# The last output tile of a gated attention and GLU kernel ends with its 128 columns instead of its 384, and the 384 leave through the phi tasks' buffer

## The chip, the cores and the metric

The kernel runs on one core of a Trainium2 chip. The metric is the device time of one execution in microseconds (us); it is shown as the median of three runs. Five engines work side by side: TensorE (PE, matrix products into PSUM), VectorE (DVE), ScalarE (ACT), GpSimd (POOL) and SyncE (SP). In this kernel SP only issues DMAs and waits for them.

## The reference

The input is `x`, 2048 tokens of width 512. The output is a mix of two branches with one gate per token:

```python
g = sigmoid((x * gate_w).sum(-1, keepdims=True))
a = attention(x)                                  # 32 heads, 4 segments of 512 tokens, see below
b = (gelu(x @ w_gate) * (x @ w_up)) @ w_down      # inner width 1792
return g * a + (1 - g) * b
```

In each segment, each head computes causal softmax attention, and a second answer read from a memory `M`, `z` summed over the earlier segments with `phi(t) = t+1 if t>0 else exp(t)`. The two are mixed by `sigmoid(beta)`, and all heads go through `wo`. All inputs and the output are bf16.

## The kernel before

The 2048 tokens are four segments `s` of 512, and each segment is four tiles of 128 tokens. A Python planner lists the work as tasks. Each task is a short run of instructions on one engine, with the buffers that it reads and writes. The order of the tasks on each engine is written out by hand in `ORDER` (lines 46 to 136), one string per engine, SP among them. The planner then plays this order with an estimated duration per instruction (`est`, and `issue` for a DMA). That play decides only two things: in which of the four `psW` PSUM banks a matmul group is placed, and in which sequence the tasks are entered when the semaphore waits are worked out. A wait that an engine has already made for the same count or a later one is dropped (lines 377 to 393).

The tasks at the end of the program, with their names:

- `downs(s)` (line 1023) makes the output of a segment. For a tile it adds up 14 matmuls with `wd` over the GLU's hidden columns `hT`, and 4 with `wo` over the attention's `oT`, into one PSUM bank. The evacuation `fin` multiplies by `omgt`, which is `1 - g` per token, into one of three staging buffers `ost`, and the DMA `out<tile>` on SP writes these 128 KB to memory. Tiles are numbered 0 to 15 over the sequence; the last segment makes 12 to 15. In its tiles 0 to 2 the `wd` part runs first, in pieces of two matmuls: `D3_2.14` and `D3_2.16` are the last two pieces of tile 14.
- Tile 15 is different (`on_x`, line 1028). Its 512 columns are split in 384 (`u = 0`) and 128 (`u = 1`), which are accumulated in the PSUM banks `X[0]` and `X[1]` (`psXALL` in the profile) that the attention no longer needs. The pieces are `D3_3w0.*` and `D3_3w1.*` for `wd`, 14 matmuls each in pieces of four (the last, `.12`, has two), and `D3_3a0.0` and `D3_3a1.0` for `wo`, four matmuls each.
- `fin3_30` (line 1048) evacuates the 384 columns on ACT into `ost[0]`, and `out15_0` writes them, 96 KB. `ost[0]` was last filled by tile 12, so `fin3_30` also waits until `out12` has landed. `fin3_31` (line 1051) evacuates the 128 columns on DVE into `obf`, and `out15_1` writes them, 32 KB in rows of 256 bytes.
- `fin3_2` (ACT, line 1065) evacuates tile 14 for `out14`. `fin3_1` (DVE, line 1068) does tile 13.
- `pex` (line 439) holds 128 x 1024 bf16. It is the scratch of the `phi_task`s (line 689), which compute `exp` for `phi`. Its last user is `pqc3_1` on DVE, for the fourth segment's queries.
- After its last DMA, SP waits for the semaphore of each output write (line 1140): those of tiles 0 to 14, then `sem_tail`, which belongs to `out15_0`, then that of `out15_1`.

In the order before, SP issues `out12 out13 out15_1 out14 out15_0`, ACT runs `fin3_0 fin3_2 fin3_30`, and DVE runs `fin3_1 fin3_31`.

Of the kernel before, what the change touches and what calls it, by code (L numbers as in the profile page):

```python
# [26 lines left out]
N_OST = 3  # L27
# [60 lines left out]
    "act": (  # L88
# [47 lines left out]
}  # L136
GAP = {DVE: 0.012, POOL: 0.063}
HOP = {PE: 0.25, ACT: 0.07, DVE: 0.07, POOL: 0.10, SP: 0.0}
# [272 lines left out]
def act_t(n, psum=True, ap=False):  # L411
    return (0.167 if psum else 0.20) + n / 1200.0 + (0.093 if ap else 0.0)


def dve_t(n, mode=1, psum=False, ap=False):
    return max(0.19, 0.155 + n / mode / 960.0 + (0.06 if ap else 0.0))
# [11 lines left out]
def _build(es, nc, A_x, A_wq, A_wk, A_wv, A_wo, A_beta, B_w_gate, B_w_up, B_w_down, gate_w, out):  # L428
    def sb(name, shape, dtype=BF):
        return es.enter_context(nc.sbuf_tensor(name, shape, dtype))  # L430
# [8 lines left out]
    pex = sb("pex", [P, 2, 512])  # L439
# [33 lines left out]
    ostage = [sb(f"ost{i}", [P, 512]) for i in range(N_OST)]  # L473
# [19 lines left out]
    def sem(name):  # L493
        nsem[0] += 1
        return es.enter_context(nc.semaphore(f"{name}_{nsem[0]}"))
# [3 lines left out]
    def task(name, eng, instrs, **kw):  # L499
        return S.add(Task(name, {eng: instrs}, **kw))  # L500

    def mm(g, view, lhsT, rhs, reads, first, last, n, fkey=None):
        return Instr(lambda e: e.matmul(view(), lhsT, rhs, start=first, stop=last),  # L503
                     reads=reads, writes=[fkey if fkey is not None else g.key], est=mm_t(n))

    def pieces(name, g, instrs, size, after=(), bias=0.0):

        r = None
        for i in range(0, len(instrs), size):
            r = task(f"{name}.{i}", PE, instrs[i:i + size], grp=g, after=after, bias=bias)  # L510
        return r
# [12 lines left out]
    def dma(name, eng, out_ap, in_ap, reads, writes, nbytes, issue=0.5, transpose=False, bias=0.0, sm=None,  # L524
            nonc=False, after=()):
        sm = sm if sm is not None else sem("d")

        def f(e):
            if transpose:
                return e.dma_start_transpose(out_ap(), in_ap())  # L530
            if nonc:
                with nc.allow_non_contiguous_dma(reason="small vector"):
                    return e.dma_start(out_ap(), in_ap())
            return e.dma_start(out_ap(), in_ap())
        return task(name, eng, [Instr(f, reads, writes, issue, dma_sem=sm)], bias=bias, nbytes=nbytes, after=after)
# [58 lines left out]
    for nm, u, k0, nk, c0 in (("0a", 0, 0, 1, 0), ("0b", 0, 1, 1, 1024), ("1", 0, 2, 2, 2048),  # L594
# [8 lines left out]
        dst = xT[0][:, k0:k0 + nk, 256 * u:256 * u + 256]  # L603
# [419 lines left out]
    def downs(s):  # L1023
        sl = s % 2
        last = s == NSEG - 1
        for tile in range(4):
            gt = 4 * s + tile
            on_x = last and tile == 3
            att = [(oT[sl][:, kb, tile * 128:(tile + 1) * 128], wo[:, kb, :], [("oT", sl, tile, kb), ("w", "wo")])
                   for kb in range(4)]  # L1030
            dwn = [(hT[sl][:, fb, tile * 128:(tile + 1) * 128], wd[:, fb, :], [("hT", sl, fb), ("w", ("wd", fb // 7))])
                   for fb in range(NFT)]
            dep = fins if on_x else ()
            if on_x:
                for part in (dwn, att):
                    for u in range(2):
                        c0, cn = 384 * u, (384, 128)[u]
                        ins = [mm(None, lambda u=u, cn=cn: X[u][:, 0:cn], a, b[:, c0:c0 + cn], rd,
                                  part is dwn and i == 0, part is att and i == 3, cn, fkey=("X", u))
                               for i, (a, b, rd) in enumerate(part)]  # L1040
                        pieces(f"D{s}_{tile}{'wa'[part is att]}{u}", None, ins, 4, after=dep)
                for u in range(2):
                    c0, cn = 384 * u, (384, 128)[u]
                    dst, dk = (ostage[(4 * s + tile) % N_OST][:, 0:cn], ("ost", (4 * s + tile) % N_OST)) if u == 0 else \
                        (obf[:, 0:cn], ("obf",))
                    rd = [("X", u), ("omgt", s)]
                    if u == 0:
                        task(f"fin{s}_{tile}{u}", ACT, [Instr(lambda e, dst=dst, u=u, cn=cn, gt=gt: e.activation(  # L1048
                            dst, X[u][:, 0:cn], ACTF.Copy, scale=omgt[:, gt:gt + 1]), rd, [dk], act_t(cn, ap=True))])
                    else:  # L1050
                        task(f"fin{s}_{tile}{u}", DVE, [Instr(lambda e, dst=dst, u=u, cn=cn, gt=gt: e.tensor_scalar(
                            dst, X[u][:, 0:cn], omgt[:, gt:gt + 1], None, ALU.mult), rd, [dk], dve_t(cn, ap=True))])
                    dma(f"out{gt}_{u}", SP, lambda gt=gt, c0=c0, cn=cn: out[0, gt * 128:(gt + 1) * 128, c0:c0 + cn],
                        lambda dst=dst: dst, [dk], [("hbm", gt, u)], 256 * cn, sm=sem_out[gt] if u else sem_tail)
                continue
            g = Grp(banks)
            key = g.key
            view = lambda g=g: g.f32()[:, :]
            seq = dwn + att if last else att + dwn
            ins = [mm(g, view, a, b, rd, i == 0, i == len(seq) - 1, 512, fkey=key)  # L1060
                   for i, (a, b, rd) in enumerate(seq)]
            pieces(f"D{s}_{tile}", g, ins, 2, after=dep)
            rd = [key, ("omgt", s)]
            f = S.add(Task(f"fin{s}_{tile}", {
                ACT: [Instr(lambda e, view=view, gt=gt, tile=tile: e.activation(
                    ostage[(4 * s + tile) % N_OST][:], view(), ACTF.Copy, scale=omgt[:, gt:gt + 1]), rd,
                    [("ost", (4 * s + tile) % N_OST)], act_t(512, ap=True))],
                DVE: [Instr(lambda e, view=view, gt=gt, tile=tile: e.tensor_scalar(  # L1068
                    ostage[(4 * s + tile) % N_OST][:], view(), omgt[:, gt:gt + 1], None, ALU.mult), rd,
                    [("ost", (4 * s + tile) % N_OST)], dve_t(512, ap=True))]}, grp=g))  # L1070
            if s == NSEG - 2:
                fins.append(f)
            dma(f"out{gt}", SP, lambda gt=gt: out[0, gt * 128:(gt + 1) * 128, :],
                lambda tile=tile: ostage[(4 * s + tile) % N_OST][:], [("ost", (4 * s + tile) % N_OST)], [("hbm", gt)], 131072, sm=sem_out[gt])

    fins = []
    sem_out = [sem("so") for _ in range(16)]
    sem_tail = sem("st")
# [17 lines left out]
    attention(1)  # L1096
    ups(0)
    downs(0)
    xdma(3)
    prep(2)  # L1100
    gelu_phase(1, [], [2])
    memory(2)
    attention(2)
    ups(1)
    downs(1)
    prep(3)
    gelu_phase(2, [], [3])
    attention(3)
    ups(2)
    downs(2)  # L1110
    ups(3)
    downs(3)
# [75 lines left out]
```

## Time and profile before

| what | value |
|---|---|
| time, median of 3 runs | 266.68 us (266.48 to 266.70) |
| profiled execution, its time | 266.81 us |
| profiled execution, its span | 265.1 us |
| DVE, ACT, POOL busy | 197.6, 209.0, 105.9 us (75%, 79%, 40%) |
| instructions on PE (matmuls, and as many weight loads) | 3153 |
| output writes | 15 of 128 KB, one of 96 KB, one of 32 KB |

The span is the stretch that the profiler shows; the time of the same execution is 1.71 us longer. In the views, a row of the timeline has its start, its duration, the engine, the source line, the operation, what it writes and what it reads, the number of instructions merged in the row, and, in brackets, how long the engine sat idle before it and which work ended that. Matmuls are recorded at line 503, whatever the task, so the tasks are told apart by their tiles and by the number in a row. Matmuls overlap, and their ends are modelled; the chain of waits gives each row of matmuls the time from the end of the one before. The issue of a DMA is a row of the SP queue, and "us to landing" counts from the start of that row.

### The profile page before, as it was taken

The page shows a single profiled execution, that of the slowest core. Times are in us where ns is not written, and L with a number is a line of the kernel's source. Part 1 is how long each engine was busy: PE and PEld are TensorE (multiplying, and loading weights), DVE is VectorE, ACT ScalarE, POOL GpSimd, SP SyncE. Part 2 cuts the span into 40 slices and gives each one's busy share as a digit, 9 for nine tenths or more (in the row PEclk, how much of TensorE's full clock was granted, in tenths as well). Part 3 has the DMA queues.
Part 4 walks back from the last instruction along what each step waited for, and adds up shares of the span by engine and source line. Part 5 has one row for each costly group of instructions (what it writes and reads, how often), then busy time and mean ns, then how long its engine had stood idle before and what let it go on. Part 6 is the DMA issues. An engine that isn't in the chain of part 4 may idle for free.

```text
span 265.1 us, 7394 instructions
## 1 busy us (share of the span) xinstructions
PE 261.1 (98%) x3153; PEld 117.5 (44%) x3153; DVE 197.6 (75%) x376; ACT 209.0 (79%) x179; POOL 105.9 (40%) x256
## 2 busy tenths in 40 slices
PE   8999999999999999999999999999999999999995
PEld 4644444344444434443544434444444433444453
DVE  0778788999997968889897776879887742466651
ACT  3698988998999788799867977878787777777611
POOL 8206686352600077174400365609470117362400
PEclk9999999999999999999999999999999999999999
DMA  7972118900003894420004251200000021301002
GB/s 224 309 182 53 33 24 197 240 4 0 2 19 102 243 160 79 63 82 0 2 0 68 67 131 21 83 2 20 5 2 0 2 63 42 79 2 42 22 0 82
DMA packets 32769, 18.25 MB, mean 69 GB/s; under 512 B 20576, under 2 KB 32736, under 8 KB 32736
## 3 DMA queue, kind: packets, MB, share of 16 engines
q1 hardware_dynamic: 31632, 16.73, 27.0%
q10 hardware_dynamic: 1104, 1.05, 1.2%
q8 instruction: 25, 0.41, 0.7%
q14 instruction: 8, 0.07, 0.1%
HBM read 9.84 MB, written 2.10 MB: 45 GB/s over the span
## 4 chain that ended last, share of the span: by engine, by line
PE 96%; ACT 1%; DMA 1%; issue 0%; ACTq 0%
PE psW L503 75%; PE psXALL L872 9%; PE psW L920 6%; PE psXALL L503 3%; PE psW L928 1%; DMA hT<-in_A_x_dram 1%; PE psW L839 1%; ACT pt L878 1%; PE psXALL L792 1%; PE psXALL L599 1%; ACT L878 0%; ACT ost L1048 0%; ACTq L399 0%
## 5 line engine op out<-in xcount | busy, mean ns | idle before, releaser
L878 ACT ACTIVATE pt<-psXALL 128x2048 bf16<-128x2048 f32 x64 | 120.1, 1876 | 27.0 <-PE psXALL L872 23.5
L881 POOL TENSOR_SCALAR_AFFINE_SELECT pt<-pt 128x256 bf16<-128x256 bf16 x128 | 58.9, 472 | 102.9 <-ACT pt L878 98.1
L503 PE MATMUL psW<-xT,wu 128*128 128x512 bf16 x224 | 55.3, 380 | 0.0
L503 PE MATMUL psW<-xT,wg 128*128 128x512 bf16 x224 | 54.2, 380 | 0.0
L503 PE MATMUL psW<-wd,hT 128*128 128x512 bf16 x210 | 54.1, 380 | 0.0
L1019 DVE TENSOR_TENSOR hT<-psW,hT 128x512 bf16<-128x512 f32 x56 | 36.8, 683 | 16.5 <-PE psW L503 16.2
L881 POOL TENSOR_SCALAR_AFFINE_SELECT ptl<-ptl 128x512 bf16<-128x512 bf16 x32 | 22.5, 704 | 38.0 <-ACT ptl L878 36.4
L503 PEld LDWEIGHTS psW<-xT,wu 128*128 128x128 bf16 x224 | 20.3, 98 | 25.7 <-issue 2.7
L503 PEld LDWEIGHTS psW<-xT,wg 128*128 128x128 bf16 x224 | 20.6, 98 | 24.7 <-issue 2.1
L934 DVE STREAM_TRANSPOSE tb<-psW 128x512 f32<-128x512 f32 x32 | 21.5, 699 | 11.7 <-PE psW L928 11.5
L503 PEld LDWEIGHTS psW<-wd,hT 128*128 128x128 bf16 x210 | 19.3, 98 | 23.9 <-issue 3.0
L872 PE MATMUL psXALL<-qT,kpad 32*128 32x320 bf16 (+3 forms) x512 | 25.4, 273 | 0.0
L1003 ACT ACTIVATE hT<-psW 128x512 bf16<-128x512 f32 x28 | 15.7, 596 | 5.5 <-PE psW L503 5.4
L503 PE MATMUL psW<-xT,wk 128*128 128x512 bf16 (+1 forms) x80 | 19.0, 342 | 0.0
L920 PE MATMUL psW<-pt,vaug 128*17 128x192 bf16 (+3 forms) x512 | 18.8, 273 | 0.0
L872 PEld LDWEIGHTS psXALL<-qT,kpad 32*128 32x128 bf16 x512 | 7.6, 92 | 24.5 <-ACT pt L878 15.4
L503 PE MATMUL psW<-wv,xT 128*128 128x512 bf16 x64 | 18.5, 380 | 0.0
L878 ACT ACTIVATE ptl<-psXALL 128x2048 bf16<-128x2048 f32 x8 | 15.0, 1876 | 3.9 <-PE psXALL L872 3.6
L503 PE MATMUL psW<-wo,oT 128*128 128x512 bf16 x60 | 17.0, 380 | 0.0
L1068 DVE TENSOR_SCALAR ost<-psW,omgt 128x512 bf16<-128x512 f32 x9 | 6.7, 746 | 11.9 <-PE psW L503 11.9
L520 DVE CAST hT<-psW 128x512 bf16<-128x512 f32 x19 | 12.8, 684 | 3.7 <-PE psW L503 3.5
L779 POOL COPY exsT<-exs 32x4 f32<-32x4 f32 x64 | 13.8, 216 | 3.6
(104 smaller groups left out, 302.2 us busy)
## 6 DMA issues: line engine op xcount, KB each, us to landing
out_dram<-ost SPq DMA_DIRECT2D x15, 128.0 KB, 1.9
wg<-in_B_w_gate_dram SPq DMA_DIRECT2D x2, 896.0 KB, 7.5
wu<-in_B_w_up_dram SPq DMA_DIRECT2D x2, 896.0 KB, 7.3
wd<-in_B_w_down_dram SPq DMA_DIRECT2D x2, 896.0 KB, 7.4
phkt<-in_A_x_dram SPq DMA_DIRECT2D x3, 512.0 KB, 4.5
vlow<-vaug SPq DMA_DIRECT2D x8, 136.0 KB, 2.8
hT<-in_A_x_dram SPq DMA_DIRECT2D x2, 256.0 KB, 3.9
wq<-in_A_wq_dram SPq DMA_DIRECT2D x2, 256.0 KB, 5.4
```

Of the source, the lines that this page charges most:

```text
L503: return Instr(lambda e: e.matmul(view(), lhsT, rhs, start=first, stop=last), reads=reads, writes=[fkey if fkey is not None else g.key], e ...
L520: alts[DVE] = [Instr(lambda e: e.tensor_copy(dst(), src()), reads=reads, writes=writes, est=dve_t(n))]
L599: task(f"x0t{nm}_{u}", PE, [Instr(lambda e, k=k, a=a, u=u, k0=k0, src=src: e.transpose(src[:, k, a * 128:(a + 1) * 128], xin[:, 2 * u + a, ...
L779: cross = task(f"exsT{s}", POOL, [Instr(lambda e, g=g, c=c: e.tensor_copy(exsT[sl][32 * g:32 * g + 32, c:16:4], exs[32 * c:32 * c + 32, s4 ...
L872: instrs.append(Instr(lambda e, g=g, lhs=lhs, rhs=rhs, c0=c0, ncol=ncol: e.matmul(X[g][:, c0:c0 + ncol], lhs(32 * g), rhs(32 * g), start=T ...
L878: exp_task(s, f"exp{s}_{t}{name}", [Instr(lambda e: e.activation(dst[:], XALL[:, :].rearrange("p (g c) -> p g c", g=4), ACTF.Exp, scale=AT ...
L881: task(f"msk{s}_{t}{name}", POOL, [Instr(lambda e, view=view, pat=pat, base=base: e.affine_select(out=view, in_=view, compare_op=ALU.is_ge ...
L920: instrs.append(Instr(lambda e, t=t, q=q, kb=kb, slot=slot, c0=c0: e.matmul(gp.f32()[32 * q:32 * q + 17, 128 * kb + 64:512], Vaug[sl][:, k ...
L934: task(f"pvt{s}_{t}_{j}", DVE, [Instr(lambda e: e.transpose(Tb[:, j, :], gp.f32()[:, :]), [gp.key], [("Tb", j)], dve_t(512))], grp=gp)
L1003: lambda e, g=g, ft=ft, s=s: e.activation(hT[s % 2][:, ft, :], g.f32()[:, :], ACTF.Gelu_apprx_tanh),
L1019: task(f"Um{s}_{ft}", DVE, [Instr(lambda e, g=g, ft=ft: e.tensor_tensor(hT[sl][:, ft, :], g.f32()[:, :], hT[sl][:, ft, :], ALU.mult), [g.k ...
L1068: DVE: [Instr(lambda e, view=view, gt=gt, tile=tile: e.tensor_scalar(ostage[(4 * s + tile) % N_OST][:], view(), omgt[:, gt:gt + 1], None, ...
```

## The change

Four things are changed.

1. On PE, the end of the order. Behind `D3_2.14` stood the last ten matmuls of the 128 columns' `wd` part, then `D3_2.16`, `D3_3a1.0`, `D3_3w0.12` and `D3_3a0.0`. Now `D3_2.16` comes first, then the rest of the 384 columns (`D3_3w0.12`, `D3_3a0.0`), then the rest of the 128 columns (`D3_3w1.4`, `.8`, `.12`, `D3_3a1.0`).
2. On SP, the end of the order: `out14`, `out15_0`, `out15_1` in place of `out15_1`, `out14`, `out15_0`.
3. `fin3_30` writes the first 384 columns of `pex` instead of `ost[0]`, and `out15_0` reads them there.
4. The planner's estimate for the issue of an output write is 0.35 us instead of 0.5.

The orders of ACT, DVE and POOL are the same, and so is each instruction's size.

```diff
         "D3_0.4 D3_0.6 qk3_3B0 U3_11.2 D3_1.2 D3_0.8 U3_12.0 U3_12.2 qk3_3A1 D3_0.10 D3_1.4 pv3_2_1 pv3_2_0 "
         "qk3_3B1 D3_1.6 D3_1.8 D3_0.12 D3_0.14 D3_1.10 D3_1.12 pv3_3_0 pv3_3_1 D3_1.14 D3_3w1.0 D3_2.0 D3_3w0.0 "
-        "D3_2.2 D3_2.4 D3_3w0.4 D3_3w0.8 D3_0.16 D3_2.6 D3_2.8 D3_1.16 D3_2.10 D3_2.12 D3_2.14 D3_3w1.4 D3_3w1.8 "
-        "D3_3w1.12 D3_2.16 D3_3a1.0 D3_3w0.12 D3_3a0.0 "),
+        "D3_2.2 D3_2.4 D3_3w0.4 D3_3w0.8 D3_0.16 D3_2.6 D3_2.8 D3_1.16 D3_2.10 D3_2.12 D3_2.14 D3_2.16 D3_3w0.12 "
+        "D3_3a0.0 D3_3w1.4 D3_3w1.8 D3_3w1.12 D3_3a1.0 "),
...
-        "oTd3_3 out10 out9 out11 out12 out13 out15_1 out14 out15_0 "),
+        "oTd3_3 out10 out9 out11 out12 out13 out14 out15_0 out15_1 "),
...
-                    dst, dk = (ostage[(4 * s + tile) % N_OST][:, 0:cn], ("ost", (4 * s + tile) % N_OST)) if u == 0 else \
+                    dst, dk = (pex[:, 0, 0:cn], ("pex",)) if u == 0 else \
                         (obf[:, 0:cn], ("obf",))
...
-                        lambda dst=dst: dst, [dk], [("hbm", gt, u)], 256 * cn, sm=sem_out[gt] if u else sem_tail)
+                        lambda dst=dst: dst, [dk], [("hbm", gt, u)], 256 * cn, issue=0.35, sm=sem_out[gt] if u else sem_tail)
...
-                lambda tile=tile: ostage[(4 * s + tile) % N_OST][:], [("ost", (4 * s + tile) % N_OST)], [("hbm", gt)], 131072, sm=sem_out[gt])
+                lambda tile=tile: ostage[(4 * s + tile) % N_OST][:], [("ost", (4 * s + tile) % N_OST)], [("hbm", gt)], 131072, issue=0.35, sm=sem_out[gt])
```

## The prediction

> **What bounds the kernel now.** I read the page first: its head, the busy times, and the engines' shares of the chain of waits.
>
> ```profile
> span 265.1 us, 7394 instructions
> PE 261.1 (98%) x3153; PEld 117.5 (44%) x3153; DVE 197.6 (75%) x376; ACT 209.0 (79%) x179; POOL 105.9 (40%) x256
> PE 96%; ACT 1%; DMA 1%; issue 0%; ACTq 0%
> ```
>
> PE works for 261.1 of 265.1 us and holds 96% of the chain. No matmul is removed, so the change can gain only behind the last one. Hence the second view, the end of the chain in order of time (start, duration, what, how many).
>
> ```profile
> 256.98 3.02 PE psW L503 x14
> 260.01 0.56 PE psXALL L503 x10
> 260.56 0.43 PE psW L503 x2
> 261.00 1.21 PE psXALL L503 x10
> 262.21 0.02 issue
> 262.23 0.04 ACTq L399
> 262.27 0.05 issue
> 262.31 0.58 ACT ost L1048
> ```
>
> The four matmul rows are, by the written order: 14 of 512 columns ending with `D3_2.14`; the ten of 128 columns (`D3_3w1.4` to `.12`), 56 ns each; the two of `D3_2.16`, 215 ns each; and ten mixed ones, `D3_3a1.0` (four of 128 columns), `D3_3w0.12` and `D3_3a0.0` (six of 384). At 56 ns the four take 0.22, which leaves 0.99/6 = 0.165 us for one of 384. PE is done at 262.21, ACT evacuates from 262.31 to 262.89. What follows is in the timeline of the same stretch, on the SP queue alone, in the DMA view (KB, us to landing), and in SP's final waits.
>
> ```profile
> 261.12 0.69 ACT L1065 ACTIVATE ost<-psW,omgt 128x512 bf16<-128x512 f32 x1 [2.89 <-PE psW L503]
> 261.26 0.35 DVE L1051 TENSOR_SCALAR obf<-psXALL,omgt 128x128 bf16<-128x128 f32 x1 [1.69 <-PE psXALL L503]
> 261.64 0.33 SPq L534 DMA_DIRECT2D out_dram<-obf  x1
> 262.01 0.43 SPq L534 DMA_DIRECT2D out_dram<-ost  x1
> 262.92 0.33 SPq L534 DMA_DIRECT2D out_dram<-ost  x1
> out_dram<-ost SPq DMA_DIRECT2D x1, 96.0 KB, 1.6
> out_dram<-obf SPq DMA_DIRECT2D x1, 32.0 KB, 1.4
> L1141 SPq EVENT_SEMAPHORE  x8: 27/28/28, 263.3 to 264.6; - x8
> ```
>
> SP issues `out15_0` at 262.92, 0.03 behind ACT's end. It lands 1.6 later, at 264.52, and SP's last wait (27 to 28 ns) is at 264.6. The program then closes until 265.1, so 0.58 lies behind the landing. From PE's end the tail is 0.10 + 0.58 + 0.03 + 1.6 + 0.58 = 2.89 us. The 128 columns, meanwhile, are evacuated at 261.26 and wait for nobody: their write lands at 261.64 + 1.4 = 263.04, 1.5 us before it is needed.
>
> **The change, part by part.**
>
> *PE's order.* The same 22 matmuls follow 260.01. `D3_2.16` runs to 260.44, the six of 384 columns to 261.43, and the fourteen of 128 at 56 ns to 262.21. Nothing is gained or lost on PE: the operands are old (the last write of `oT`, the second row below, ends at 256.35), and each group stays in its bank. The unknown is whether fourteen short matmuls in a row keep the pace of ten. The bound from below is 56 ns; the one from above is a weight load that isn't covered, 98 ns by the first row below, which for the four added ones makes 4 x 0.042 = 0.17 us. I take zero, because the run of ten is the nearest row.
>
> ```profile
> L503 PEld LDWEIGHTS psXALL<-wd,hT x11: 97/98/98, 259.8 to 261.1; 128*128 128x128 bf16 x11
> 255.93 0.42 DVE L954 TENSOR_TENSOR oT<-oT,ott 128x512 bf16<-128x512 bf16 x1
> ```
>
> The Trainium skill speaks against this order: "TensorE: Matmul & The Clock Gate", section "Back-to-back issue gap", gives about 81 ns for each matmul of 128 columns in a sustained stream with weight loads. By it, an estimate, PE would be 14 x 25 ns = 0.35 us later; the run of ten measured 56 ns, so the trace does not agree, and the sum goes without it.
>
> *The last evacuation.* It passes from ACT to DVE. DVE's `fin3_31` began at 261.26, 0.04 behind the end of `D3_3a1.0` (261.00 + 0.22), and takes 0.35. In place of 0.10 + 0.58 that is 0.39, a gain of 0.29. The two hops differ because ACT's row has a wait of its own in the queue (0.04) and DVE's hasn't; nothing in `fin3_31`'s waits changes. If DVE's hop were ACT's, the gain would be 0.23. After: 262.21 + 0.39 = 262.60, issue at 262.63 with the same 0.03.
>
> *The last write.* 32 KB in 1.4 us instead of 96 KB in 1.6: gain 0.2, and 0.1 to 0.3 with the rounding of both. SP's last wait is now the one for the last landing, where before one more stood behind it: 0.03 for that row, at most 0.08 with the gap to 264.6; I take 0.05.
>
> Here, too, the skill warns: "DMA: Bandwidth & Descriptors", section "Specifications", has writes under 512 bytes a descriptor done by read-modify-write, and these rows are 256 bytes. The rates below bear the direction out (94 GB/s at a share of 0.43 against 197 at 0.61), yet the whole 32 KB still landed earliest.
>
> ```profile
> 262.40:262.75 0.35, 0.00 (x0) 0.00 (x0) 0.00 (x0) 0.35 (x1) 0.00 (x0) 1.00 0.43 94
> 263.70:264.20 0.50, 0.00 (x0) 0.00 (x0) 0.00 (x0) 0.00 (x0) 0.00 (x0) 1.00 0.61 197
> ```
>
> *What is moved ahead must be out of the way.* Three issues now stand in front of `out15_1` on SP. `fin3_2` starts 0.12 behind 260.44 as it did behind 261.00, ends at 261.25, and `out14` is issued from 261.28 to 261.71 at the longer 0.43. `fin3_30` starts by 261.53, ends by 262.11, and `out15_0` is issued from 262.14 to 262.47, or 262.57 at 0.43. `out15_1` is ready at 262.63: SP is free with 0.06 to 0.16 to spare. That slack is the cover of the two issues; a delay of `fin3_30` beyond it costs one for one. `out15_0` lands at 263.74 and `out15_1` at 264.03, so the later landing is the 32 KB.
>
> *The idle buffer.* The issue rows of `out12` and `out13`, each with its time to landing:
>
> ```profile
> 258.25 0.33 SPq L534 DMA_DIRECT2D out_dram<-ost  x1
> out_dram<-ost SPq DMA_DIRECT2D x1, 128.0 KB, 3.9
> 259.60 0.33 SPq L534 DMA_DIRECT2D out_dram<-ost  x1
> out_dram<-ost SPq DMA_DIRECT2D x1, 128.0 KB, 2.9
> L702 DVE TENSOR_TENSOR phq<-phq,pex x1: 694/694/694, 175.3 to 175.3; 128x1024 bf16<-128x1024 bf16 x1
> ```
>
> `out12` lands at 262.15. In `ost[0]`, `fin3_30` could not start before that, 0.62 later than it now may, and SP would hold `out15_1` behind `out15_0` (262.15 + 0.10 + 0.58 + 0.03 + 0.33 = 263.19 instead of 262.63, +0.56: the whole gain). `pex` was last read at 175.3 + 0.69, before work that ACT has waited for since, so its new wait costs nothing. Before, this wait was hidden by 0.06 us under PE's end; moving to `pex` alone gains no more than that.
>
> *The planner's 0.35.* It issues no instruction. It could only move a group to another bank in the middle, where an eviction is 0.69 (ACT) or 0.75 us (DVE) long. I take zero, with bounds of minus and plus 0.7: the output writes do not set the planned start of any task on another engine but `fin3_30`, so I expect the same program up to 260.01.
>
> **Sum.** 0.29 + 0.20 + 0.05 = 0.54 us. The tail is 0.39 + 0.03 + 1.4 + 0.53 = 2.35 instead of 2.89, and the span 264.56. The profiled execution's 266.81 becomes 266.27; it lies 0.13 above the median of 266.68, which becomes **266.14**. A measurement of this kernel can tell about 0.2% from no change, 0.53 us, so the line is at 266.15 and the forecast almost on it.
>
> **The rivals.**
>
> *The writes collide on SP or in the DMA engines* (chance 0.08). `out15_1` follows 96 KB by 0.49. For it: SP's slack of 0.06 is thin. Against it: `out10` and `out9`, twice 128 KB and 0.4 apart, landed in 1.7 to 1.8.
>
> ```profile
> L534 SPq DMA_DIRECT2D out_dram<-ost x2: 337/384/431, 241.5 to 241.9; - x2
> DMA to landing us min/median/max: 1.7/1.8/1.8
> ```
>
> A landing of 1.8 instead of 1.4 gives 266.54; a tenth lost in SP's queue gives 266.24.
>
> *The short matmuls slow down* (0.06). Unhidden loads on the four added ones give 266.14 + 0.17 = 266.31; by the skill's rate, that of 81 ns on all fourteen, it would be 266.49.
>
> *Slower: a late DMA engine catches the last write* (0.06). The two slow landings have a cause in these windows of the DMA queues and of the engines:
>
> ```profile
> q8 instruction: 1, 0.02, 55.2%
> 259.20:260.90 1.70, 1.70 (x18) 1.11 (x17) 0.37 (x1) 0.00 (x0) 0.00 (x0) 1.00 0.43 136
> 260.90:262.10 1.20, 1.20 (x11) 0.65 (x9) 0.35 (x1) 0.69 (x1) 0.00 (x0) 1.00 0.06 14
> 262.10:262.40 0.30, 0.09 (x1) 0.00 (x0) 0.00 (x0) 0.09 (x1) 0.00 (x0) 1.00 0.00 0
> ```
>
> One instruction packet between 259.1 and 259.3 takes 55.2% of 16 engines for 0.2 us, that is 1.77 us of one engine; then about one engine (0.06 of 16) drags 14 GB/s behind it until 262.1. If that happened under `out15_1`, a landing of 2.9 like `out13`'s gives 266.14 + 1.5 = 267.64. It costs time from a landing of 1.4 + 0.54 = 1.94 on. Against it: the packet comes before the first changed instruction, and the drag is over at 262.1, half a us ahead of the new last issue.
>
> *The plan shifts after all* (0.04): some banks in the middle change, 265.4 to 266.8.
>
> **How the numbers follow.** The forecast has 0.76. Its own range, from the 0.23 of the hop, the 0.1 to 0.3 of the landing and the spread of the three runs (0.2), is 265.95 to 266.35. Being on the line it splits: 0.45 faster by more than 0.2%, 0.31 within. The plan adds 0.03 to faster and 0.01 to slower; collision and slow matmuls (0.14) fall within; the late engine (0.06) is slower. Faster 0.48, same 0.45, slower 0.07. The range reaches over the collision's 266.54 to 266.55 and starts at 265.95, which leaves out the late engine and most of a shifted plan.
>
> **What would show it.** Right: up to 260.01 the same chain; PE's last row 0.78 us for 14 matmuls, ending at about 262.2; then DVE L1051, not ACT, as the last compute row, from 262.25 for 0.35; `out15_0` issued near 262.1 and reading `pex`; `out15_1` at 262.63, landing in 1.4; a span near 264.56. Wrong: SP still issuing `out15_0` after 262.6; a last landing above 1.6; PE's end past 262.3; ACT's L1048 starting later than 261.6; another `psW` stall in the middle; or an instruction packet on the DMA queues after 261.

## The result, and the profile after

| | median | executions | ratio to before |
|---|---|---|---|
| before | 266.75 us (266.48 to 268.55) | 22 | |
| after | 266.27 us (265.94 to 266.77) | 22 | 0.9973 [0.9962, 0.9985] |

The medians differ by 0.48 us, the fastest executions by 0.54, the lower quartiles (266.60 and 265.99) by 0.61. Some executions of before took 267 or 268 us, and such an execution, seen in e9_before below, lost its time at the start; the ratio, with these late executions in it, amounts to 0.72 us, and its interval to 0.40 to 1.01. The profiled execution of after took 266.56 us. The head and the busy times of its page:

```profile
span 264.8 us, 7355 instructions
PE 256.1 (97%) x3115; PEld 117.9 (45%) x3153; DVE 197.5 (75%) x376; ACT 209.0 (79%) x179; POOL 105.7 (40%) x256
```

The span is only 0.3 us shorter than before's 265.1. (PE's busy time is 5 us less only because 38 matmul records are missing: 3115 beside 3153 weight loads.) The end of the chain, which answers to the eight rows of before:

```profile
257.21 3.45 PE psW L503 x16
260.66 1.77 PE psXALL L503 x20
262.43 0.02 issue
262.46 0.35 DVE obf L1051
```

The pieces have moved as written: `D3_2.16` has joined the 512-column row, and the 20 matmuls of tile 15 stand last, 6 x 0.165 + 14 x 0.056 = 1.77 us. DVE's L1051 has taken ACT's place. But PE ends at 262.43, not 262.21. The timeline of the stretch, and from the DMA view the two last writes, show the rest:

```profile
260.78 0.69 ACT L1065 ACTIVATE ost<-psW,omgt 128x512 bf16<-128x512 f32 x1 [2.33 <-PE psW L503]
261.49 0.33 SPq L534 DMA_DIRECT2D out_dram<-ost  x1
261.67 0.58 ACT L1048 ACTIVATE pex<-psXALL,omgt 128x384 bf16<-128x384 f32 x1 [0.21 <-PE psXALL L503]
262.28 0.33 SPq L534 DMA_DIRECT2D out_dram<-pex  x1
262.84 0.33 SPq L534 DMA_DIRECT2D out_dram<-obf  x1
```

```profile
out_dram<-pex SPq DMA_DIRECT2D x1, 96.0 KB, 1.6
out_dram<-obf SPq DMA_DIRECT2D x1, 32.0 KB, 1.4
L1141 SPq EVENT_SEMAPHORE  x8: 28/28/28, 263.2 to 264.3; - x8
```

From PE's end to the end of the span there were 265.1 - 262.21 = 2.89 us before, and there are 264.8 - 262.43 = 2.37 now, 0.52 less. The other 0.22 were lost long before the tail, in the first 7 us. The chain of before and then that of after there:

```profile
6.03 0.22 PE psXALL L599 x4
6.26 0.44 PE psW L503 x4
6.69 0.22 PE psXALL L599 x4
```

```profile
6.02 0.43 PE psXALL L599 x4
6.44 0.48 PE psW L503 x4
6.92 0.22 PE psXALL L599 x4
```

The same four transposes of the input took 0.22 and 0.43 us, and from there PE ran about 0.2 us late. This stretch of the program is the same in both. The last row of attention scores shows that nothing in between made the lag larger; it is quoted from the timeline of before and from that of after:

```profile
248.67 0.40 PE L872 MATMUL psXALL<-qT,kpad 32*128 32x320 bf16 x8
```

```profile
248.89 0.40 PE L872 MATMUL psXALL<-qT,kpad 32*128 32x320 bf16 x8
```

It is 0.22 later, and PE's end is 13.54 us behind it in both. So two lengths are read from each trace below: from that row to PE's end, and the tail from PE's end to the span's end. They are free of the run's start, which the times are not.

### The profile page after: what moved, and what is told of

Read it like the earlier page. It is cut to its first block, busy times and chain, and to the rows that moved or that the text cites. A ratio compares the mean times of both kernels' runs of the same rounds, so it can differ in the third digit from the quotient of the medians.

```text
span 264.8 us, 7355 instructions
## 1 busy us (share of the span) xinstructions
PE 256.1 (97%) x3115; PEld 117.9 (45%) x3153; DVE 197.5 (75%) x376; ACT 209.0 (79%) x179; POOL 105.7 (40%) x256
## 4 chain that ended last, share of the span: by engine, by line
PE 91%; DVE 3%; issue 2%; DMA 1%; ACT 1%; DVEq 0%; ACTq 0%
PE psW L503 71%; PE psXALL L872 8%; PE psW L920 5%; PE psXALL L503 3%; DMA hT<-in_A_x_dram 1%; PE psW L928 1%; PE psW L839 1%; DVE hT L520 1%; ACT pt L878 1%; PE psXALL L599 1%; PE psXALL L792 1%; ACT L878 0%; DVE kpad L738 0%; DVE pex L700 0%; DVE phq L698 0%
## 5 line engine op out<-in xcount | busy, mean ns | idle before, releaser
L503 PE MATMUL psW<-xT,wu 128*128 128x512 bf16 x217 | 53.9, 380 | 0.9 <-issue 0.6
L503 PE MATMUL psW<-wd,hT 128*128 128x512 bf16 x204 | 52.8, 380 | 1.0 <-issue 0.8
L503 PE MATMUL psW<-xT,wg 128*128 128x512 bf16 x214 | 52.1, 379 | 1.4 <-issue 0.8
L503 PE MATMUL psW<-wv,xT 128*128 128x512 bf16 x61 | 17.8, 380 | 0.5 <-issue 0.3
L503 PE MATMUL psW<-wo,oT 128*128 128x512 bf16 x54 | 15.4, 380 | 1.0 <-issue 0.8
```

## The experiments

Each kernel ran 11 or 12 times (after 22 times), in turn with the kernel before on the same chip. "Q1" is the lower quartile of a kernel less that of before from the same job; the median and the ratio hold more of the late executions. PE's end is the start of the issue row behind the last matmul; in e1, whose chain does not pass there, it is the end of the last matmuls in the timeline (261.57 + 0.39). Times in us.

| kernel | median, before's | ratio [interval] | Q1 | PE's end | span | tail |
|---|---|---|---|---|---|---|
| before (profile) | | | | 262.21 | 265.1 | 2.89 |
| after | 266.27, 266.75 | 0.9973 [0.9962, 0.9985] | -0.61 | 262.43 | 264.8 | 2.37 |
| e0_again | 266.38, 266.98 | 0.9972 [0.9947, 0.9996] | -0.53 | 262.63 | 265.0 | 2.37 |
| e1_ost | 266.70, 266.98 | 0.9979 [0.9955, 1.0003] | -0.22 | 261.96 | 264.9 | 2.94 |
| e2_pex | 266.71, 266.98 | 0.9970 [0.9946, 0.9994] | -0.08 | 262.37 | 265.2 | 2.83 |
| e3_spold | 267.44, 266.98 | 1.0003 [0.9980, 1.0026] | +0.55 | 261.86 | 265.4 | 3.54 |
| e4_pe_old | 266.88, 266.82 | 1.0008 [0.9991, 1.0026] | +0.17 | 262.07 | 265.1 | 3.03 |
| e5_256 | 266.28, 266.82 | 0.9974 [0.9959, 0.9989] | -0.36 | 262.15 | 264.7 | 2.55 |
| e6_448 | 266.42, 266.82 | 0.9995 [0.9973, 1.0016] | -0.21 | 261.92 | 264.6 | 2.68 |
| e7_act448 | 266.55, 266.65 | 0.9989 [0.9974, 1.0003] | -0.15 | 262.02 | 264.7 | 2.68 |
| e8_act416 | 266.36, 266.65 | 0.9980 [0.9959, 1.0000] | -0.44 | 261.95 | 264.4 | 2.45 |
| e9_before | 266.68, 266.90 | 0.9993 [0.9979, 1.0008] | -0.03 | 263.21 | 266.1 | 2.89 |
| e10_after | 266.35, 266.90 | 0.9981 [0.9967, 0.9996] | -0.56 | 261.96 | 264.3 | 2.34 |

From the start of the last attention scores to PE's end it is 13.53 to 13.54 us in all thirteen traces. No order or cut of tile 15 changed what PE needs; behind that row the traces differ in the tail alone.

**e0_again and e10_after: the changed kernel again.**

> The changed kernel once more, beside the kernel before on the same chip. Theory (the gain is the shorter tail behind PE's last matmul): 0.54 us less in the medians, and in the profile a tail of 2.35 to 2.40 us from PE's end to the span's end, whatever the start of the run was. Rival (the 0.72 us of the first comparison's ratio holds gain that the tail has not): the medians differ by 0.7 or more again.

> The changed kernel a third time, beside the kernel before under both names. Theory: 0.5 to 0.6 us less than before in the medians and in the lower quartile, against either name. Rival (a gain of 0.7 or more beyond the tail): 0.7 or more less than both.

The tails are 2.37 and 2.34, although PE's end lies 0.67 us apart in the two traces; e10's run had a short start, and its span is 264.3. The medians are 0.60 and 0.55 below before, Q1 0.53 and 0.56. Against e9_before, the kernel before under its other name in e10's job, the median is only 0.33 lower, and Q1 0.52. So the theory holds in the tails and the lower quartiles, though not in every median. The medians ask for no gain beyond the tail; the ratios amount to 0.75 and 0.51 us and move with the late executions.

**e9_before: the kernel before, against itself.**

> The kernel before, unchanged, compared with itself. Theory (the ratio's 0.72 us holds some executions of before that began late and that the tail has nothing to do with): the comparison shows a ratio of 0.998 to 0.999 here too, because the baseline's executions hold more late ones, and the median and the lower half agree within 0.1 us. Rival (the changed kernel really has fewer late executions): a ratio of 1.000, with as many late executions on both sides.

The ratio is 0.9993 with 1 inside its interval, nearer to the rival than to the theory, and the late executions are as frequent on both sides (4 of 12 above 267 us here, 7 of 23 beside it). Yet the medians differ by 0.22 and Q1 by 0.03: a median of 12 or 23 executions of the same kernel moves by 0.2 us. This kernel's profile caught a late execution. A row of its PE timeline and the end of its chain:

```profile
8.30 0.92 PE L503 MATMUL psW<-xT,wk 128*128 128x256 bf16 x7 [1.21 <-DMA wk<-in_A_wk_dram]
```

```profile
262.00 1.21 PE psXALL L503 x10
263.21 0.02 issue
263.23 0.04 ACTq L399
263.27 0.05 issue
263.32 0.58 ACT ost L1048
```

PE stood 1.21 us for a weight that landed late, and its end is 1.0 later than in the first profile, yet the tail is the same 2.89. Such executions are what the 267 and 268 us of before are likely to be; how often they fall on which kernel stays open.

**e1_ost: the buffer undone.**

> The changed kernel with the 384 columns back in ost[0], so that their evacuation waits for the landing of out12. Theory: ACT's L1048 starts at that landing, which was 3.4 us behind the issue in the trace of after and 3.9 in the one of before, so 0.3 to 0.6 later than in the changed kernel, and SP holds the last write behind it: 0.1 to 0.56 us longer than the changed kernel, 0 to 0.45 less than before. Rival (the buffer is immaterial, out12 has landed by then): the same as the changed kernel, 0.54 less than before.

```diff
-                    dst, dk = (pex[:, 0, 0:cn], ("pex",)) if u == 0 else \
+                    dst, dk = (ostage[(4 * s + tile) % N_OST][:, 0:cn], ("ost", (4 * s + tile) % N_OST)) if u == 0 else \
```

The end of its chain:

```profile
258.01 3.78 DMA out_dram<-ost
261.79 0.03 ACTq L399
261.81 0.04 issue
261.86 0.58 ACT ost L1048
```

The chain now runs back through the landing of `out12`, 3.78 us, and no longer through PE. On the SP queue `out15_0` and `out15_1` are issued one right behind the other:

```profile
262.46 0.33 SPq L534 DMA_DIRECT2D out_dram<-ost  x1
262.84 0.43 SPq L534 DMA_DIRECT2D out_dram<-obf  x1
out_dram<-obf SPq DMA_DIRECT2D x1, 32.0 KB, 1.6
```

The last row is from the DMA view: the last write lands in 1.6 in place of 1.4. The tail is 2.94, so in this trace all that the new orders gain is lost again. In the times about half of it is lost (Q1 -0.22 instead of -0.53). A likely reason is that the landing of `out12` varies, 3.2 to 3.9 us in these traces; the executions without a trace do not show it.

**e2_pex: the buffer alone.**

> The kernel before with the buffer alone: the 384 columns leave through pex, the orders stay as before. Theory: the landing of out12 was hidden by 0.06 us under PE's end, so 0 to 0.08 less than before (0.06 if also ACT's own wait row of 0.04 goes). Rival (the evacuation waited for out12 in unprofiled runs): 0.2 or more less than before.

```profile
262.37 0.02 issue
262.40 0.58 ACT pex L1048
```

These are the last rows of its chain: ACT starts 0.03 behind PE where it took 0.10, as its own wait row is gone. The tail is 2.83, 0.06 less. Q1 says 0.08 less, the median 0.27, which the control above cannot tell from the late executions. The ratio, 0.9970, is even as low as that of the changed kernel in the same job (0.9972): 17 of the 35 executions of before took more than 267 us there. So the ratios do not separate the two kernels, and against the rival speak the tail and Q1 alone.

**e3_spold: SP's order undone.**

> The changed kernel with SP's order of before (out15_1, out14, out15_0). Theory: SP waits for the 128 columns first, issues them at 262.63 on the clock of before, then out14 and out15_0 at 263.0 and 263.4, and the last landing is that of 96 KB at 265.0: 0.45 to 0.55 us longer than before, 1.0 longer than the changed kernel. Rival (the order on SP hardly matters, since the writes overlap in the DMA engines): within 0.2 of the changed kernel.

```diff
-out13 out14 out15_0 out15_1
+out13 out15_1 out14 out15_0
```

```profile
262.26 0.33 SPq L534 DMA_DIRECT2D out_dram<-obf  x1
262.64 0.43 SPq L534 DMA_DIRECT2D out_dram<-ost  x1
263.12 0.43 SPq L534 DMA_DIRECT2D out_dram<-pex  x1
out_dram<-pex SPq DMA_DIRECT2D x1, 96.0 KB, 1.7
```

SP's queue shows three issues behind PE's end (261.86) where after has one; the last row is the landing of the last write. The tail is 3.54, 0.65 above before's and 1.17 above after's, somewhat more than expected because the issues in a row took 0.43 and the last write 1.7; the times agree in Q1 at +0.55, and the median is 1.06 above that of e0_again in the same job.

**e4_pe_old: PE's order undone.**

> The changed kernel with PE's order of before (384 columns last), with SP's new order and pex. Theory: ACT's evacuation is last again, out15_0 is issued as before and the finished 128 columns stand behind it, issued 0.37 later with 1.4 to landing: 0.17 later landing, less 0.05 for the final waits and 0 to 0.06 for the buffer: 0.05 to 0.15 us longer than before. Rival (the gain is that 384 and 96 KB are issued earlier on SP, not that the 128 are last): shorter than before.

```profile
262.70 0.33 SPq L534 DMA_DIRECT2D out_dram<-pex  x1
263.07 0.43 SPq L534 DMA_DIRECT2D out_dram<-obf  x1
```

The 128 columns, evacuated from 261.12 on in this trace, are issued at 263.07, behind the 384. The tail is 3.03, 0.14 longer than before, as expected. So each of PE's order, SP's order and the buffer is needed: with any one undone, the tail in the trace is 2.94 or more.

**e5_256: a cut in two halves.**

> The changed kernel with tile 15 cut in 256 and 256 columns. Theory: the sum on PE is nearly the same (0.11 us a matmul); the last evacuation grows by 128 columns at 0.96 per ns, 0.13 us, and the last write of 64 KB lands in 1.5: 0.2 to 0.25 longer than the changed kernel, 0.3 less than before. Rival (rows of 256 bytes cost more than rows of 512): the write lands in 1.4 or less and only the evacuation's 0.13 is lost.

```diff
-                    c0, cn = 384 * u, (384, 128)[u]
+                    c0, cn = 256 * u, (256, 256)[u]
```

The last evacuation and its issue, from the timeline, and the landing, from the DMA view:

```profile
262.18 0.48 DVE L1051 TENSOR_SCALAR obf<-psXALL,omgt 128x256 bf16<-128x256 f32 x1 [3.09 <-PE psXALL L503]
262.69 0.33 SPq L534 DMA_DIRECT2D out_dram<-obf  x1
out_dram<-obf SPq DMA_DIRECT2D x1, 64.0 KB, 1.5
```

0.13 more on DVE and 0.1 more in the landing, and 0.18 in the tail: rows of 512 bytes did not land sooner than 32 KB in rows of 256. The medians do not tell the two cuts apart.

**e6_448 and e7_act448: a smaller last part, and the same with ACT's own DMA queue.**

> The changed kernel with tile 15 cut in 448 and 64 columns. Theory: DVE's evacuation falls to 0.28 and the last landing to 1.3 to 1.4, a gain of 0.1 to 0.15, but matmuls of 64 columns don't get below about 0.05 us because each needs its weight load, while those of 448 take 0.19: PE ends 18 x (0.19 + 0.05 - 0.22) = 0.36 later, so about 0.2 us longer than the changed kernel. Rival (a matmul costs its columns): PE's end stays, and it is 0.1 to 0.15 shorter than the changed kernel.

> The cut in 448 and 64 columns again, with out15_0 issued from ACT's own queue, right behind its evacuation. Theory (that cut lost its gain on SP, where the 64 columns stood behind out15_0): the last write is issued 0.33 behind PE's end instead of 0.65; the 112 KB, issued 0.3 behind PE's end, now land last, 1.7 later: tail 0.3 + 1.7 + 0.53 = 2.5 to 2.55 us instead of 2.70, still longer than the 2.38 of the changed kernel. Rival (the 128-byte rows of the last write cost the time): the tail stays at 2.70.

The first theory fell. Rows of e6's chain, then of its timeline:

```profile
253.23 0.12 PE psXALL L503 x4
260.36 1.56 PE psXALL L503 x20
261.92 0.03 issue
261.94 0.28 DVE obf L1051
```

```profile
261.53 0.63 ACT L1048 ACTIVATE pex<-psXALL,omgt 128x448 bf16<-128x448 f32 x1 [0.37 <-PE psXALL L503]
262.19 0.33 SPq L534 DMA_DIRECT2D out_dram<-pex  x1
262.57 0.43 SPq L534 DMA_DIRECT2D out_dram<-obf  x1
```

Four matmuls of 64 columns take 0.12, 0.03 each (of 128, 0.056), so a matmul does cost its columns here, and PE ends as ever. The tail is longer all the same, 2.68: the 448 columns are ready only at 262.16, and the finished 64 (262.22) wait for SP until 262.57. In e7 ACT issues the large write:

```profile
262.30 0.39 ACTq L534 DMA_DIRECT2D out_dram<-pex  x1
out_dram<-pex ACTq DMA_DIRECT2D x1, 112.0 KB, 1.8
```

The small one goes out at 262.35, 0.33 behind PE's end, but the tail stays 2.68. That is the rival's number, but not its reason: the 16 KB land at about 263.95 (1.6 behind their issue), and the 112 KB behind them at 264.10, in 1.8 where 1.7 was expected. What the 128-byte rows cost by themselves stays open.

**e8_act416: a try at a shorter version.**

> A cut in 416 and 96 columns, with out15_0 issued from ACT's queue: a try at a version shorter than the changed kernel. Theory: both writes are out of each other's way, the 104 KB issued 0.08 behind PE's end and landing at 1.78, the 24 KB issued at 0.37 and landing at 1.77: a tail of 2.3 us instead of 2.38, so about 0.6 less than before. Rival (a second queue, or a DMA issued by ACT, adds its own cost): a tail of 2.4 or more.

```profile
262.02 0.37 ACTq L534 DMA_DIRECT2D out_dram<-pex  x1
262.32 0.33 SPq L534 DMA_DIRECT2D out_dram<-obf  x1
```

```profile
out_dram<-pex ACTq DMA_DIRECT2D x1, 104.0 KB, 1.7
out_dram<-obf SPq DMA_DIRECT2D x1, 24.0 KB, 1.6
```

Both issues come when expected, but the 24 KB take 1.6 to land instead of 1.4, and the tail is 2.45, the rival's figure. In after, the 32 KB are issued 0.56 behind the 96 KB and take 1.4; here the smaller write follows by 0.30. On SP's queue alone, 32 KB that followed the 96 KB by 0.37 and 0.38 took 1.5 (e4) and 1.6 (e1), so the short distance would do as a reason without the second queue; no run separates the two. By its tail the changed kernel's cut remains the shortest of those tried.

## Why the prediction was right

The time lies in the range, and the mechanism is the predicted one. The range alone would show little: 265.95 to 266.55 holds gains from 0.13 to 0.73 us, so the account rests on the tails. Two of the prediction's signs of being wrong did appear, PE's end past 262.3 (262.43) and L1048 later than 261.6 (261.67). Both come from the 0.22 us of the start; without it they are 262.21 and 261.45. Step by step:

- *PE's order costs nothing.* Right: 1.77 us for the last 20 matmuls, of which 14 x 0.056 = 0.78 for the short ones, and 13.54 us from the last attention scores, as before. "TensorE: Matmul & The Clock Gate" of the Trainium skill, "Back-to-back issue gap", would have had 81 ns; no run here shows it, and the rival of slow matmuls is out.
- *The last evacuation*, predicted at 0.39: 262.43 to 262.81, 0.38.
- *The last write*, predicted at 1.4 and 0.53 behind it: issued 0.41 behind PE's end, landed by 264.24, then 0.56. The tail of 2.35 measured 2.37, 2.37 and 2.34.
- *SP's slack*, predicted at 0.06 to 0.16, was 0.23 (free at 262.61, issue at 262.84), since ACT starts 0.02 to 0.03 behind PE without its own wait row. (Two issues were moved ahead of `out15_1`, `out14` and `out15_0`, not three.) The collision did not come here; e6 shows it, where `out15_0` was ready later.
- *The buffer.* Predicted: alone up to 0.06, and without it the whole gain lost, 0.56. Measured in the tails: 0.06 (e2) and 0.57 (e1). Both numbers agree partly by luck. The 0.06 of e2 is not time spent waiting for `out12`, which had landed before PE's end, but the wait's own row on ACT: without it the start moved from 0.10 to 0.03 behind PE. In e1 the last issue came 0.88 behind PE's end instead of 0.98, and its landing took 1.6 instead of 1.4.
- *The planner's 0.35.* With 0.5 put back, the built program is the same byte for byte, so it is no part of the gain.
- *The late engine.* `out12` again took 3.4 us, but the drag was over before the last writes, as argued: from 261.85 to 262.30 the DMA engines' share was 0.00.

The forecast of 266.14 is 0.13 below the measured median. Of this, 0.06 is the gain (0.48 in the medians instead of 0.54), and 0.07 is before itself, which measured 266.75 here instead of the 266.68 that the forecast started from. Both are within what the start of the run moves. Apart from e9 with its late weight, PE's end lies between 261.86 (e3) and 262.63 (e0), with the first profile of before in the middle, and the medians of before lie between 266.65 and 266.98. The 0.2% line of 0.53 us, put through the middle of the forecast, could not be decided: the medians differ by 0.48, 0.60 and 0.55, and the ratios (0.27%, 0.28% and 0.19%) have the line inside their intervals.

## What to carry to other kernels

When one engine is busy to the end, the end of the program is its own small problem: the tail is the hop, the last evacuation, the issue, the landing and the final waits, so let a small and quickly evacuated piece be last on every queue at once. It need not be the smallest: with 64 and 96 columns last, the larger write ahead came too late or too close, and the tails were 2.68 and 2.45. A reordering pays only as a set: here, with PE's order, the DMA queue's order or the early free buffer missing, the whole gain was gone from the traced tail (without the buffer, about half of it from the times). For half a microsecond in 266, measure the tail from a mark inside the trace, because the start of the run scatters by as much.

## What the runs showed that was not expected

- The first transposes and matmuls ran at two speeds in the same program, though the windows show a granted clock of 1.00 there: four transposes in 0.22 or 0.43 us (before, after), and the rest of the run moved by it.
- An ACT evacuation with a wait row of its own started 0.10 behind PE (before), without it 0.02 to 0.03 (after, e2).
- A matmul of 64 columns took 0.03 us in e6, beside weight loads that the rows give as 98 ns: ten of these loads took 0.52 us together, so they overlap each other too.
- The landing of a small write went with its distance from the one ahead: 32 KB took 1.4 us at 0.55 behind 96 KB (after, e0, e10), 1.5 at 0.37 (e4) and 1.6 at 0.38 (e1).
